# Hedgehog linear attention and Mish layers on one core: first key tiles' sums in twos, block 1's features loaded in stage one, -mean x rstd on GpSimd, statistics behind low parts, fold copies ahead of low parts

## The chip, the cores and the metric

The kernel runs on one core of a Trainium2 chip. The metric is device time in microseconds (us) of one execution; lower is better. The core has TensorE (PE, matmuls), VectorE (DVE), ScalarE (ACT), GpSimd (POOL) and SyncE (SP, which here only issues DMAs). Each engine works through its own queue in order and waits at an instruction until what that instruction needs is there.

## The reference

Two layers, each an attention and a dense block with residuals; 2048 rows of width 640, 32 heads of 20, hidden width 1536, all float32:

```python
for _ in range(2):
    x = x + A(layernorm(x))
    x = x + B(layernorm(x))

def A(x):                      # hedgehog linear attention
    q, k, v = heads(x @ wqkv)
    pq, pk = q @ w_phi, k @ w_phi            # per head, 20 x 20
    phi_q = concat(softmax(pq), softmax(-pq))
    phi_k = concat(softmax(pk), softmax(-pk))
    kv = phi_k.T @ v ; z = sum over rows of phi_k
    return ((phi_q @ kv) / (phi_q @ z + 1e-6)) @ wo

def B(x):                      # dense, Mish, dense
    h = x @ w1 + b1
    return (h * tanh(softplus(h))) @ w2
```

Both layers use the same weights.

## The kernel before

**Numbers.** Matmul operands are split into a high part (rounded to fp32r by an ACT copy) and a low part (the rest, by a subtraction on DVE or GpSimd), and each product is three matmuls: high x high, high x low, low x high. In the profile `xth`/`xtl` are the parts of the transposed rows, `r1h`/`r1l` and `r2h`/`r2l` those of weights.

**Stages.** A layer has three, and TensorE runs through them in turn. Stage one of attention (`attend_first`; about 0 to 246 us in layer 0, 704 to 907 in layer 1) takes the rows in 8 blocks of 256, two tiles of 128 each, tiles 0 to 15. For each tile it makes keys, values and queries by generators (`keys`, `values`, `queries`): a projection of 30 matmuls (L414), an ACT copy out of PSUM, then `features`. That is the two softmaxes: a maximum and a minimum on DVE, two subtractions (one on GpSimd for queries, L440), an exponential on ACT, a row sum and a reciprocal on DVE, and the product with the reciprocal on GpSimd (L450), called the norm product below. From the keys' features and the values (with a column of ones) come the sums phi_k^T V, 32 heads, in a PSUM tile `kva` (L491). Queries' features are transposed on DVE and stored by SP to DRAM, `e_d` (L508), four DMAs per tile. Stage two (`attend_second`) loads `e_d` back (L720, L725), averages (L768), transposes the averages on TensorE (L334, into PSUM tiles called `one`), projects with wo and adds. The dense stage has the two dense products (L892, L943) and the Mish between them.

**Before the first block** of layer 0 the weights of w_phi are folded into those of the keys: `fold_phi` makes pairs of groups on TensorE (L263), and each group's `fold_end` is an ACT copy (`fold_high`, L279) and a DVE subtraction (`fold_low`, L283), group by group.

**Buffers.** Keys' features and loaded `e_d` blocks share a ring of five `big` tiles; pairs of row tiles share a ring of six named `ol`; a query tile is one of two buffers (`r` with number 210 or 211, tile i in i mod 2), which the query tile two later reuses once the store of the former has landed. The first instruction to do so is a small memset (L430) on GpSimd at the head of `features`, or the ACT copy. PSUM has four `one` tiles and two `mm` pairs.

**What sets the order.** A generator's `yield` hands the turn back, and `advance()` gives each pending generator one step, so that the sums of a key tile fall some projections behind its own. In `keys` one more `yield` in the middle blocks puts a block's first tile together with its second, so that 64 heads are summed in one go; the first two and the last blocks sum tile by tile. Inside `written()` and `manual_schedule` instructions stand as the code has them; elsewhere a scheduler orders them within what `tc.issue_after(x)` demands, which is that an instruction stands behind x. `last_low`, `last_sub`, `last_fold` and the like hold such an x: the latest low part, subtraction, fold subtraction. The rows of a block in layer 0 get their layernorm statistics by `norm_stats` (DVE) and `norm_scale` (GpSimd, and -mean x rstd on DVE, L319). In layer 1 these come with the dense stage before; only low parts (L351, on GpSimd there) are left.

**At the end of stage one** `load(0)` and parts of block 1 (`load_groups(1, 0)`, `load_end(1)`) are loaded; `load_groups(1, 5)`, the other half of block 1, is loaded inside stage two, between the stores of query tiles 12 and 13. Query tile 15's copy out of PSUM comes in stage two as well, as the projections left over (`rest`).

Of the kernel before, what the change touches and what calls it, by code (L numbers as in the profile page):

```python
# [8 lines left out]
F32 = mybir.dt.float32  # L9
# [7 lines left out]
P = 128  # L17
S = 2048
D = 640
# [25 lines left out]
def kernel(  # L45
# [45 lines left out]
    for _ in range(30):  # L91
# [25 lines left out]
    last_act, in_written, last_low, last_load, last_recip, last_fold, last_product, last_sub = (  # L117
        [None], [False], [None], [None], [None], [None], [None], [None])
# [20 lines left out]
    def v_tile():  # L139
        return work.tile([P, VW], F32, tag="v", name="v", bufs=2)  # L140

# [144 lines left out]
    def fold_end(ws, ps, k, c):  # L286
        fold_high(ws, ps, k, c)
        fold_low(ws, ps, k, c)

    def fold_phi(ws, bd, raw, parts):  # L290

        for n in range(0, len(parts), 2):
# [6 lines left out]
            for (k, c), ps in pair:  # L299
                fold_end(ws, ps, k, c)  # L300
# [11 lines left out]
    def norm_scale(b, mvs):  # L312

        ve = work.tile([P, BT], F32, tag="ve", name="ve", bufs=2)
        for t in range(BT):
            nc.gpsimd.tensor_scalar(ve[:, t:t + 1], mvs[t][:, 1:2], LN_EPS, 1.0, op0=ALU.add, op1=ALU.mult)
# [108 lines left out]
    def features(ps, e, pool_sub, scale=nc.gpsimd):  # L425
# [23 lines left out]
        last_recip[0] = nc.vector.reciprocal(r, r).ins  # L449
        ins = scale.tensor_tensor(eg, eg, r.unsqueeze(2).to_broadcast([P, 2 * H, DH]), op=ALU.mult).ins  # L450
# [9 lines left out]
    def attend_first(layer, x_src, first):  # L460


        def fetch_normed(b):
# [3 lines left out]
            with (tc.issue_after((last_fold if b == 3 else last_sub)[0]) if b in (1, 3) else nullcontext()):  # L467
# [3 lines left out]
        pending = []  # L471

# [7 lines left out]
        def keys(xts, i, v):  # L480
            e = big_tile()
            yield from features(project(xts, i % BT, kv_ws, 0, w=QC), e, False,
                                nc.vector if i == NT - 1 else nc.gpsimd)
            yield
            if i % BT == 0 and BT < i < NT - BT:
                yield
            for r in range(9):
                for j in range(4):
                    h = 3 * (4 * (r // 3) + j) + r % 3
                    if h < H:  # L490
                        nc.tensor.matmul(kva[32 * j:32 * j + DH + 1, 40 * r:40 * r + 40],  # L491
                                         v[:, (DH + 1) * h:(DH + 1) * (h + 1)], e[:, 40 * h:40 * h + 40],
                                         start=(i == 0 and r == 0), stop=(i == NT - 1), skip_group_check=True)

        def queries(xts, i, ps=None):
# [11 lines left out]
            for q in range(4):  # L507
                nc.sync.dma_start(dst[t, q], e[32 * q:32 * q + 32].rearrange("f (j s) -> f j s", s=32))  # L508
# [3 lines left out]
        def values(xts, i, v):  # L512
            vv = v.rearrange("p (h d) -> p h d", d=DH + 1)
            act(vv[:, :, DH], ident[:, :H], AF.Copy, scale=0.0, bias=1.0)
            if i < BT:
                pv = project(xts, i, kv_ws, D, [one_tile(), one_tile()])
                for c in range(2):
                    act(vv[:, c * H // 2:(c + 1) * H // 2, :DH],
                        pv[c][:, :HC].rearrange("p (h d) -> p h d", d=DH), AF.Copy)
            else:  # L520
                pv = project(xts, i % BT, kv_ws, D)
                act(vv[:, :, :DH].rearrange("p (c h) d -> p c h d", c=2),
# [103 lines left out]
        for b in range(NB):  # L626
# [10 lines left out]
            vs = [v_tile() for _ in range(BT)]  # L637
# [4 lines left out]
            for n, (kind, t) in enumerate(order):  # L642
# [66 lines left out]
        return kva, o_ws, loaded, begun, xs, rest()  # L709
# [5 lines left out]
    def load_groups(b, g0):  # L715
# [5 lines left out]
        return [t[:, g * BLK:(g + 1) * BLK] for g in range(5)]  # L721

# [21 lines left out]
    def attend_second(x_src, x_dst, acc, fetches, makes, fetch_next, begin_next):  # L744
        kva, o_ws, loaded, begun, xs, rest = acc
# [60 lines left out]
        with tc.manual_schedule(engines={mybir.EngineType.PE, mybir.EngineType.SP}):  # L806
            kv = finish_kv(kva)
            next(rest)
            next(kv)
            loaded[1] = begun[0] + load_groups(1, 5) + begun[1]  # L810
# [5 lines left out]
            loaded[2] = load(2)  # L816
# [300 lines left out]
```

## Time and profile before

| | us |
|---|---|
| median of 3 runs | 1357.31 (1357.02 to 1357.4) |
| the profiled execution | 1357.15 |
| its span, first to last instruction | 1355.4 |
| TensorE busy | 1347.9 |
| stage one / two / dense, layer 0 | about 0-250 / 250-356 / 356-704 |
| the same, layer 1 | about 704-911 / 911-1015 / 1015-1356 |

A row of the timeline reads: start, duration, engine, line, operation, result<-operands, shapes, count, and in brackets how long the engine stood idle before it and what ended that. `SPq` rows are issues of DMAs by SP. TensorE overlaps its matmuls: they start closer together than they last.

### The profile page before, as it was taken

To read this page: it belongs to the slowest core of one execution; us is meant where nothing else is said; L and a number is where in the kernel's file an instruction comes from. 1 tells how busy PE (TensorE), PEld (TensorE's weight loads), DVE (VectorE), ACT (ScalarE), POOL (GpSimd) and SP (SyncE) were. 2 spreads that over 40 slices of the span, in tenths; PEclk is the share of its full clock that TensorE was granted. 3 is DMA by queue.
4 is the path that set the end of the run, shared out by engine and by line. 5 is a ranking of instruction groups with operands and counts; after the bars stand their busy time and mean duration, and the time that the engine had idled before them with its cause. 6 is when DMAs were issued, how large, how long until landed. Compare 5 with 4: busy or idle time off the path is not lost.

```text
span 1355.4 us, 30982 instructions
## 1 busy us (share of the span) xinstructions
PE 1347.9 (99%) x12896; PEld 1337.4 (99%) x12896; DVE 1061.2 (78%) x1799; ACT 575.7 (42%) x968; POOL 462.4 (34%) x417
## 2 busy tenths in 40 slices
PE   9999999999999999999999999999999999999999
PEld 9999999999999999999999999999999999999998
DVE  6888988886787887778769788788768776676775
ACT  5444444212454545445443334332236444444443
POOL 3355544334222222222225655634251211111112
PEclk9999999999999999999999999999999999999999
DMA  9544444698714442244474534548974221233200
GB/s 332 166 101 92 95 111 99 173 289 280 216 35 95 117 118 71 61 104 104 140 231 100 122 79 90 95 102 263 282 259 127 79 68 41 88 98 98 70 29 20
DMA packets 352629, 174.11 MB, mean 128 GB/s; under 512 B 287449, under 2 KB 324041, under 8 KB 352489
## 3 DMA queue, kind: packets, MB, share of 16 engines
q1 hardware_dynamic: 352489, 172.14, 46.9%
q8 instruction: 101, 1.65, 0.5%
q14 instruction: 39, 0.32, 0.1%
HBM read 106.23 MB, written 65.86 MB: 127 GB/s over the span
## 4 chain that ended last, share of the span: by engine, by line
PE 94%; DVE 2%; DMA 2%; POOL 1%; SPq 1%; ACT 0%; issue 0%; POOLq 0%; ACTq 0%
PE mm L414 26%; PE one L892 25%; PE mm L943 24%; PE one L414 12%; PE mm L768 2%; PE one L334 2%; PE one L491 1%; PE one L943 1%; DMA xt<-in_x 1%; PE one L768 1%; DVE r L448 1%; DMA raw<-in_wqk_t 0%; DVE m L439 0%; DMA v<-in_wv 0%; DVE r L442 0%; SPq L508 0%
## 5 line engine op out<-in xcount | busy, mean ns | idle before, releaser
L943 PE MATMUL mm<-r2h,ol 128*128 128x320 f32 x1240 | 296.1, 309 | 0.0
L918 POOL TENSOR_TENSOR ol<-big,ol 128x512 fp32r<-128x512 f32 (+1 forms) x98 | 131.1, 1338 | 477.7 <-ACT ol L917 419.5
L892 PE MATMUL one<-xtl,r1h 128*128 128x256 f32 x960 | 268.2, 279 | 0.0
L892 PE MATMUL one<-xth,r1l 128*128 128x256 f32 x960 | 268.0, 279 | 0.0
L892 PE MATMUL one<-xth,r1h 128*128 128x256 f32 x960 | 265.9, 279 | 0.0
L943 PEld LDWEIGHTS mm<-r2h,ol 128*128 128x128 f32 x1240 | 212.5, 188 | 0.0
L943 PE MATMUL mm<-r2l,ol 128*128 128x320 f32 x620 | 191.2, 309 | 0.0
L414 PE MATMUL mm<-r1h,xth 128*128 128x304 f32 (+1 forms) x600 | 185.2, 309 | 0.0
L414 PE MATMUL mm<-r1l,xth 128*128 128x304 f32 (+1 forms) x600 | 183.7, 306 | 0.0
L414 PE MATMUL mm<-r1h,xtl 128*128 128x304 f32 (+1 forms) x600 | 183.6, 306 | 0.2 <-POOL xtl L351 0.2
L892 PEld LDWEIGHTS one<-xtl,r1h 128*128 128x128 f32 x960 | 180.4, 188 | 0.0
L892 PEld LDWEIGHTS one<-xth,r1l 128*128 128x128 f32 x960 | 180.4, 188 | 0.0
L892 PEld LDWEIGHTS one<-xth,r1h 128*128 128x128 f32 x960 | 179.6, 188 | 0.0
L907 DVE TENSOR_SCALAR big<-big 128x512 f32<-128x512 f32 (+1 forms) x98 | 57.2, 583 | 110.0 <-ACT big L905 109.8
L909 ACT ACTIVATE big<-big,two 128x512 f32<-128x512 f32 (+1 forms) x98 | 70.1, 715 | 116.1 <-DVE big L908 116.1
L917 ACT ACTIVATE ol<-big 128x512 fp32r<-128x512 f32 (+1 forms) x98 | 60.9, 622 | 137.6 <-DVE big L916 137.4
L905 ACT ACTIVATE big<-one,b1s 128x256 f32<-128x256 f32 x192 | 80.9, 468 | 89.0 <-PE one L892 88.5
L450 POOL TENSOR_TENSOR r<-r,r 128x1280 f32<-128x1280 f32 x32 | 77.2, 2413 | 118.9 <-DVE r L449 100.8
L943 PEld LDWEIGHTS mm<-r2l,ol 128*128 128x128 f32 x620 | 116.4, 188 | 0.0
L414 PEld LDWEIGHTS mm<-r1h,xth 128*128 128x128 f32 x600 | 112.8, 188 | 0.9
L414 PEld LDWEIGHTS mm<-r1h,xtl 128*128 128x128 f32 x600 | 112.8, 188 | 0.4 <-POOL xtl L351 0.4
L414 PEld LDWEIGHTS mm<-r1l,xth 128*128 128x128 f32 x600 | 112.8, 188 | 0.1
(161 smaller groups left out, 3142.7 us busy)
## 6 DMA issues: line engine op xcount, KB each, us to landing
e_d<-r SPq DMA_DIRECT2D x128, 160.0 KB, 4.2
big<-e_d SPq DMA_DIRECT2D x32, 640.0 KB, 8.0
x_d<-xt SPq DMA_DIRECT2D x23, 640.0 KB, 4.8
xt<-x_d SPq DMA_DIRECT2D x22, 640.0 KB, 5.3
n_d<-xn SPq DMA_DIRECT2D x168, 80.0 KB, 2.3
xt<-in_x SPq DMA_DIRECT2D x16, 640.0 KB, 4.4
xn<-x_d SPq DMA_DIRECT2D x28, 320.0 KB, 4.4
v<-n_d SPq DMA_DIRECT2D x30, 256.0 KB, 3.0
```

What stands on the lines that cost most here:

```text
L334: nc.tensor.transpose(ps[:, c, t * P:(t + 1) * P], self.rows[t][:, (c0 + c) * P:(c0 + c + 1) * P], ident)
L414: last_product[0] = nc.tensor.matmul(ps[:, :w], a[:, sl], r, start=(k == 0 and n == 0), stop=(k == KD - 1 and n == 2)).ins
L448: nc.vector.tensor_reduce(r, eg, axis=AX.X, op=ALU.add)
L450: ins = scale.tensor_tensor(eg, eg, r.unsqueeze(2).to_broadcast([P, 2 * H, DH]), op=ALU.mult).ins
L768: nc.tensor.matmul(po[c][64 * q:64 * q + 64, GW * j:GW * j + w], phs[g][:n, s0:s0 + 64], kvb[:n, g, :w], start=True, stop=True)
L892: nc.tensor.matmul(ph[:, j, :], l, r, start=(n == 0), stop=(n == 3 * KD - 1))
L905: exps[0] = nc.scalar.activation(part(ta, 0)[:, j - js.start], ph[:, j, :], AF.Exp, bias=b1s[:, 2 * pr + j:2 * pr + j + 1]).ins
L907: nc.vector.tensor_scalar_min(e, e, E_CAP)
L909: nc.scalar.activation(r, n, AF.Ln, bias=two)
L917: nc.scalar.activation(ah[:, js], n, AF.Copy)
L918: nc.gpsimd.tensor_tensor(al[:, js], n, ah[:, js].bitcast(F32), op=ALU.subtract)
L943: ins = nc.tensor.matmul(pys[t][c][:, :HC], (ah, ah, al)[n][:, j, t * P:(t + 1) * P], w, start=(f == 0 and n == 0), stop=(f == KF - 1 and ...
```

## The change

Five edits. (1) The sums of the first two blocks are also made for two tiles at once: `held(i)` gives the number of extra `yield`s for tile i. For this the values of block 0 (layer 0) and of block 2 (layer 1) come in two halves out of the `ol` ring (`v_halves`), written by two copies each. (2) The features of block 1 are loaded wholly in stage one, one big tile and three `ol` tiles (`load_rest`), and block 2's load stands behind the last store of tile 13 (`last_store`). (3) -mean x rstd is a `tensor_scalar` on GpSimd outside `written()`. (4) In `fold_phi` both high copies stand ahead of both subtractions. (5) The next block's statistics stand behind the last low part; in block 1 of layer 1 the keys' features take one more `yield`, and their norm product stands behind the low parts (`late`).

```diff
@@ features, keys
+        if late:
+            yield
         r = work.tile([P, 2 * H], F32, tag="r", name="r", bufs=2)
...
-        ins = scale.tensor_tensor(eg, eg, r.unsqueeze(2).to_broadcast([P, 2 * H, DH]), op=ALU.mult).ins
+        with (tc.issue_after(last_low[0]) if late else nullcontext()):
+            ins = scale.tensor_tensor(eg, eg, r.unsqueeze(2).to_broadcast([P, 2 * H, DH]), op=ALU.mult).ins
...
-            with (tc.issue_after((last_fold if b == 3 else last_sub)[0]) if b in (1, 3) else nullcontext()):
+            with tc.issue_after((last_sub if b == 1 else last_low)[0]):
                 norm_scale(b, [norm_stats(t, xt) for t in range(BT)])
...
+        def held(i):
+
+            b, t = divmod(i, BT)
+            if layer and b == 1:
+                return (3, 2)[t]
+            if b == 1 or (b == 0 and not layer):
+                return (2, 0)[t]
+            return int(t == 0 and b < NB - 1)
...
-                                nc.vector if i == NT - 1 else nc.gpsimd)
+                                nc.vector if i == NT - 1 else nc.gpsimd, layer and i // BT == 1)
             yield
-            if i % BT == 0 and BT < i < NT - BT:
+            for _ in range(held(i)):
                 yield
+            opens = not summed[0]
+            summed[0] = True
...
-                                         v[:, (DH + 1) * h:(DH + 1) * (h + 1)], e[:, 40 * h:40 * h + 40],
-                                         start=(i == 0 and r == 0), stop=(i == NT - 1), skip_group_check=True)
+                                         v[1][c][:, (DH + 1) * g:(DH + 1) * (g + 1)], e[:, 40 * h:40 * h + 40],
+                                         start=(opens and r == 0), stop=(i == NT - 1), skip_group_check=True)
@@ values
-            vs = [v_tile() for _ in range(BT)]
+            vs = [v_halves(b == 2 * layer) for _ in range(BT)]
+    def v_halves(apart):
+
+        if apart:
+            return None, [pair_tile(F32).rearrange("p a s -> p (a s)")[:, :VW // 2] for _ in range(2)]
+        v = v_tile()
+        return v, [v[:, :VW // 2], v[:, VW // 2:]]
@@ norm_scale, fold_phi
-            nc.vector.scalar_tensor_tensor(stats[:, b, 1, t:t + 1], mvs[t][:, 0:1], -1.0,
-                                           stats[:, b, 0, t:t + 1], op0=ALU.mult, op1=ALU.mult)
+            (nc.vector if in_written[0] else nc.gpsimd).tensor_scalar(
+                stats[:, b, 1, t:t + 1], mvs[t][:, 0:1], stats[:, b, 0, t:t + 1], -1.0, op0=ALU.mult, op1=ALU.mult)
...
-            for (k, c), ps in pair:
-                fold_end(ws, ps, k, c)
+            for end in (fold_high, fold_low):
+                for (k, c), ps in pair:
+                    end(ws, ps, k, c)
@@ loads
-                    begun = load_groups(1, 0), load_end(1)
+                    loaded[1] = load_groups(1, 0) + load_rest(1)
+    def load_rest(b):
+
+        out = []
+        for g0 in (5, 7, 9):
+            t = pair_tile(F32)
+            n = min(2, 10 - g0)
+            src = e_d[b][120 * g0:120 * (g0 + n - 1) + P]
+            src = bass.AP(tensor=src.tensor, offset=src.offset, ap=[[BLK, P], [120 * BLK, n], [1, BLK]])
+            nc.sync.dma_start(t[:, :n], src)
+            out += [t[:, 0], t[:, 1]]
+        nc.sync.dma_start(t[:80, 1], e_d[b][1200:])
+        return out
...
             next(rest)
+            with tc.issue_after(last_store[0]):
+                loaded[2] = load(2)
             next(kv)
-            loaded[1] = begun[0] + load_groups(1, 5) + begun[1]
             next(kv)
             next(rest)
             average(0, 0)
             average(0, 1)
             next(rest)
-            loaded[2] = load(2)
```

Lines of the changed kernel are some 4 to 34 higher than those of the kernel before (L279 becomes L286, L351 L355, L430 L434, L440 L444, L450 L457, L508 L528, L720 L741, L725 L759).

How the order moves at three places. First ACT at the weights' fold of layer 0 (`r1h0` to `r1h3` are the high copies, `xn` the rows normalised for block 1, `v` and `ol` the values), before:

```order
L279 ACTIVATE r1h0_166<-mm_420 128x342
L279 ACTIVATE r1h2_170<-mm_431 128x342
L279 ACTIVATE r1h1_168<-mm_420 128x342
L135 ACTIVATE xn_442<-xt_198,stats_113 128x640
L135 ACTIVATE xn_443<-xt_198,stats_113 128x640
L135 ACTIVATE v_358<-ident_70 128x32
L135 ACTIVATE v_358<-one_447 128x16x20
L279 ACTIVATE r1h3_172<-mm_431 128x342
```

and after:

```order
L286 ACTIVATE r1h0_166<-mm_423 128x342
L286 ACTIVATE r1h1_168<-mm_423 128x342
L286 ACTIVATE r1h2_170<-mm_434 128x342
L286 ACTIVATE r1h3_172<-mm_434 128x342
L135 ACTIVATE xn_445<-xt_198,stats_113 128x640
L135 ACTIVATE xn_446<-xt_198,stats_113 128x640
```

The fourth copy moves from behind the normalisations to ahead of them.

Second, SP where stage one of layer 0 goes over into stage two (`e_d0`, `e_d1` and so on are the blocks in DRAM; `r210` and `r211` hold query tiles 12 and 13), before:

```order
L720 DMA big_3113<-e_d0_116 128x5x256
L720 DMA big_3117<-e_d1_117 128x5x256
L508 DMA e_d6_122<-r210_2829 32x40x32 x4
L720 DMA big_3298<-e_d1_117 128x5x256
L508 DMA e_d6_122<-r211_2874 32x40x32 x4
L720 DMA big_3386<-e_d2_118 128x5x256
```

and after:

```order
L741 DMA big_3117<-e_d0_116 128x5x256
L741 DMA big_3121<-e_d1_117 128x5x256
L528 DMA e_d6_122<-r210_2833 32x40x32 x4
L528 DMA e_d6_122<-r211_2878 32x40x32 x4
L741 DMA big_3305<-e_d2_118 128x5x256
L741 DMA big_3307<-e_d2_118 128x5x256
```

The load between the two stores is gone; the other half of block 1 is among the loads far ahead of this place.

Third, GpSimd in blocks 1 and 2 of layer 1 (`xtl` low parts; `r210`, `r211` query tiles; `big_9235`, `big_9307` and in the other kernel `big_9242`, `big_9282` the keys of block 1; `big_9607`, and `big_9584` and `big_9624`, those of block 2), before:

```order
L450 TENSOR_TENSOR r211_9184<-r211_9184,r_9422 128x1280
L351 TENSOR_TENSOR xtl_9433<-xn_9229,xth_9431 128x512
L450 TENSOR_TENSOR big_9235<-big_9235,r_9469 128x1280
L430 MEMSET r210_9482 128x32
L351 TENSOR_TENSOR xtl_9480<-xn_9231,xth_9478 128x512
L450 TENSOR_TENSOR big_9307<-big_9307,r_9516 128x1280
L351 TENSOR_TENSOR xtl_9522<-xn_9233,xth_9520 128x256
L440 TENSOR_TENSOR r210_9482<-r210_9482,m_9558 128x32x20
```

and after:

```order
L457 TENSOR_TENSOR r211_9191<-r211_9191,r_9429 128x1280
L355 TENSOR_TENSOR xtl_9440<-xn_9236,xth_9438 128x512
L434 MEMSET r210_9485 128x32
L355 TENSOR_TENSOR xtl_9483<-xn_9238,xth_9481 128x512
L457 TENSOR_TENSOR big_9242<-big_9242,r_9519 128x1280
L355 TENSOR_TENSOR xtl_9525<-xn_9240,xth_9523 128x256
L457 TENSOR_TENSOR big_9282<-big_9282,r_9566 128x1280
L444 TENSOR_TENSOR r210_9485<-r210_9485,m_9561 128x32x20
```

The memset of the query tile is now the second of these behind `r211`, and the two norm products of the keys are behind the second and the last low part. In block 2, after:

```order
L355 TENSOR_TENSOR xtl_9833<-xn_9580,xth_9831 128x512
L457 TENSOR_TENSOR big_9584<-big_9584,r_9758 128x1280
L434 MEMSET r210_9835 128x32
L457 TENSOR_TENSOR big_9624<-big_9624,r_9869 128x1280
L355 TENSOR_TENSOR xtl_9875<-xn_9582,xth_9873 128x256
```

The second norm product stands behind a memset and ahead of the last low part; before, the last low part was ahead of it.

More of the change, by code (lines that the diff above doesn't have):

```diff
@@ L423, in query_tile, with features @@
         return r2_wide(10 + i % 2, F32).rearrange("p s d -> p (s d)")
-    def features(ps, e, pool_sub, scale=nc.gpsimd):
+    def features(ps, e, pool_sub, scale=nc.gpsimd, late=False):
         eg = e.rearrange("p (g d) -> p g d", d=DH)
@@ L707, in rest @@
                 advance()
-        return kva, o_ws, loaded, begun, xs, rest()
+        return kva, o_ws, loaded, xs, rest()
     def load(b):
```

28 lines of the change are left out of this document (14 added, 14 removed).

## The prediction

> **What bounds the kernel now.** I read the page's header first, then the chain of waits, then the list of what TensorE waited for, then the windows by stage.
>
> ```profile
> span 1355.4 us, 30982 instructions
> PE 1347.9 (99%) x12896; PEld 1337.4 (99%) x12896; DVE 1061.2 (78%) x1799; ACT 575.7 (42%) x968; POOL 462.4 (34%) x417
> PE 94%; DVE 2%; DMA 2%; POOL 1%; SPq 1%; ACT 0%; issue 0%; POOLq 0%; ACTq 0%
> PE one L334 <- ACT r L135: 1.8, 2, 1.3
> PE mm L263 <- DVE r1l L283: 0.4, 1, 0.4
> PE mm L414 <- POOL xtl L351: 0.2, 1, 0.2
> 0.00:250.00 250.00, 248.04 (x2756) 244.61 (x2758) 208.18 (x306) 108.92 (x168) 116.21 (x115) 1.00 0.54 141
> 356.00:704.00 348.00, 348.00 (x2665) 348.00 (x2664) 280.01 (x487) 175.10 (x310) 82.09 (x81) 1.00 0.42 110
> ```
>
> TensorE is the bound: 1347.9 of 1355.4 us busy, and 94% of the chain that ended last. The next three rows list waits (us in total, times, longest); the last two are windows (length, then busy time of PE, weight loads, DVE, ACT, POOL, then the granted clock, 1.00). The first dense stage has no idle microsecond at all, so nothing that moves there can gain. Only two things shorten this kernel: fewer or cheaper TensorE instructions, and the waits in the list. The change takes up three of its entries, 2.4 us together, and the cost of four switches between two shapes of matmul. An edit on another engine counts only where it makes TensorE wait.
>
> **The weights' fold.** Both ACT copies of a pair of groups now stand ahead of both DVE low parts.
>
> ```profile
> 29.73 0.46 ACT L279 ACTIVATE r1h<-mm 128x342 fp32r<-128x342 f32 x1 [2.14 <-DVE r1l L283]
> 30.09 1.72 ACT L135 ACTIVATE xn<-xt,stats 128x640 f32<-128x640 f32 x2
> 32.15 0.45 ACT L279 ACTIVATE r1h<-mm 128x342 fp32r<-128x342 f32 x1
> 32.63 0.52 DVE L283 TENSOR_TENSOR r1l<-mm,r1h 128x342 fp32r<-128x342 f32 x1 [1.40 <-ACT r1h L279]
> 33.29 0.64 PE L263 MATMUL mm<-big,raw 120*128 120x114 f32 x4 [0.38 <-DVE r1l L283]
> ```
>
> The third copy (29.73) waited 2.14 us for a low part, so two normalisations (1.72 us) slipped ahead of the fourth (32.15); its low part ended at 33.15 and the matmul that takes its buffer lost 0.38. With the four copies in a row the fourth ends some 4 us earlier, far ahead of TensorE. A stall also breaks the overlap of matmuls, which start 0.14 apart and last 0.30 (next fence): another 0.16. So **0.54 saved**; bounds 0.38 and 0.54. The normalisations slip by two copies (0.9 us) and TensorE needs their result only in block 1.
>
> **The sums in twos.** A group of sums stands between projections, single (64 instructions) or for two tiles (128):
>
> ```profile
> 725.97 0.30 PE L414 MATMUL mm<-r1h,xtl 128*128 128x304 f32 x1
> 726.21 0.83 PE L491 MATMUL one<-big,v 128*21 128x40 f32 x64
> ...
> 727.22 0.31 PE L414 MATMUL mm<-r1l,xth 128*128 128x320 f32 x1
> ...
> 776.12 0.30 PE L414 MATMUL mm<-r1l,xth 128*128 128x304 f32 x1
> 776.26 0.30 PE L414 MATMUL mm<-r1h,xtl 128*128 128x304 f32 x1
> 776.49 1.48 PE L491 MATMUL one<-big,v 128*21 128x40 f32 x128
> ...
> 778.14 0.30 PE L414 MATMUL mm<-r1l,xth 128*128 128x304 f32 x1
> ```
>
> From the last projection before to the second behind pass 1.25 us for a single and 1.88 for a pair. Either stretch holds two ordinary steps of 0.14, so the excursion costs 0.96 or 1.60, and a merge of two singles saves 2 x 0.96 - 1.60 = 0.32. Layer 0 merges twice: **0.64**. Layer 1 merges twice, but its second pair is parted again, 9 instructions at one place and the rest 16 projections on, which gives one merge back: **0.32**. The Trainium skill says the same of the direction (TensorEngine Tiling (Array Packing), Key Properties): changing the tiling mode drains TensorE. Its rule has no figure, and the rows give 0.32.
>
> The later sums must not wait for their products. In layer 0 the second pair moves ahead to about 86.3 us, since its place is 423 projections into the stage. GpSimd's queue there holds the product row below, which ended at 87.12 against a single sum at 87.7; three small statistics and a memset (2.0 us in all) leave its way, so I put it at 85.1 to 85.4: a slack of about 0.9 us, and no wait.
>
> ```profile
> 84.75 2.37 POOL L450 TENSOR_TENSOR big<-big,r 128x1280 f32<-128x1280 f32 x1
> ```
>
> The values' halves cost ACT two more copies of ones and, in layer 1, one more copy of values per tile. ACT is 42% busy and such copies are under 0.8 us: nothing.
>
> **The stage boundary of layer 0.** This is the largest term.
>
> ```profile
> 236.05 3.34 SPq L508 DMA_DIRECT2D e_d<-r  x4
> 245.27 0.38 SPq L720 DMA_DIRECT2D big<-e_d  x1
> 245.75 7.23 SPq L508 DMA_DIRECT2D e_d<-r  x4
> 243.30 1.50 DVE L503 STREAM_TRANSPOSE r<-r 128x1280 f32<-128x1280 f32 x1
> 255.44 0.74 ACT L135 ACTIVATE r<-one 128x304 f32<-128x304 f32 x2 [5.16 <-DMA e_d<-r]
> 253.55 1.09 PE L334 MATMUL one<-ident,xn 128*128 128x128 f32 x8
> 255.92 0.44 PE L334 MATMUL one<-ident,xn 128*128 128x128 f32 x2 [1.28 <-ACT r L135]
> 256.71 0.69 DVE L351 TENSOR_TENSOR xtl<-one,xth 128x512 fp32r<-128x512 f32 x1 [1.48 <-ACT xth L135]
> ```
>
> The last query tile's copy (ACT, 255.44) overwrites the buffer of tile 13 and waited 5.16 us for that tile's store; TensorE's ninth transpose needs the PSUM tile that this copy frees, 0.48 us later. Tile 13 was transposed at 244.80, but its four stores stood on SP behind a load of block 1's features (245.27), which itself waits for the last pair of sums, and shared the DMA engines with it: 7.23 us to issue instead of 3.34. The change takes that load away; block 1's features come in during the stage, in one big tile and four smaller DMAs of the same bytes, and block 2's load stands behind the stores.
>
> Now the first store issues at about 244.85. If it lands 9.7 us later as here (245.75 to 255.44), the transpose starts at 255.03; if the issue takes 3.9 us less, at 251 or so, which is no limit. The eight transposes cost (1.09 - 0.27)/7 = 0.117 each from start to start (0.27 the length of one), so the ninth could start at 254.49. The gain is 0.89 to 1.43; I take **1.43**, as the store at 236.05, without a load ahead, is the nearest row. DVE's 1.48 idle goes with it, and it is the engine that the next TensorE work follows.
>
> **The same place in layer 1.**
>
> ```profile
> 906.75 5.75 SPq L508 DMA_DIRECT2D e_d<-r  x4
> 916.49 0.44 PE L334 MATMUL one<-ident,xn 128*128 128x128 f32 x2 [0.53 <-ACT r L135]
> ```
>
> Here 0.53 + 0.16 = **0.69** can go; the stores begin only some 0.2 us earlier, so the low bound is 0.2, the high one 0.69 with the shorter issue.
>
> **Layer 1's stage one: GpSimd.** Here the change also costs.
>
> ```profile
> 742.38 0.68 ACT L135 ACTIVATE r<-mm 128x608 f32<-128x608 f32 x1 [3.93 <-DMA e_d<-r]
> 746.72 0.74 POOL L351 TENSOR_TENSOR xtl<-xn,xth 128x256 fp32r<-128x256 f32 x1
> 747.51 0.41 PE L414 MATMUL mm<-r1h,xtl 128*128 128x304 f32 x1 [0.15 <-POOL xtl L351]
> 769.97 0.55 DVE L449 RECIPROCAL r<-r 128x64 f32<-128x64 f32 x1
> 771.47 2.37 POOL L450 TENSOR_TENSOR big<-big,r 128x1280 f32<-128x1280 f32 x1
> ```
>
> Block 2's last low part ended at 747.46 behind two norm products; TensorE lost 0.15 + 0.16 = 0.31. Now only one product stands ahead of it, but so does the query tile's memset, which waits for a store that landed by 742.38 (ACT waited for the same). Taking a landing near 741.3 (the DVE work ahead of its transpose gets about 1 us shorter): low part 1.29, product 2.37, low part 0.74, ready at 745.8. TensorE has passed three singles here before, one pair now, 2.88 - 1.60 = 1.28, and asks at 747.36 - 1.28 = 746.1. So **0.31 saved**; with the landing at 742.38 it is 0.7 late, and nothing is saved.
>
> What is late next: both keys' products of block 1 follow, the second ends near 748.2 and the queries' subtraction behind it starts 0.8 us later than now; and in block 2 DVE takes both reciprocals only behind both reductions and transposes. I work the first to 769.8, near the row at 769.97. GpSimd then needs two products, start to start 2.33, and between them a memset that waits for a store: ready at about 774.5. The row above ended at 773.84, and TensorE asked at 776.49. It now asks 16 projections earlier (2.24), one excursion of 0.64 and the 0.31 less: 773.2. A **new wait of 1.1**; bounds 0 and 2.4 (both products as now, or a store as late as the row at 742.38).
>
> **Statistics.** They move behind low parts, and -mean x rstd to GpSimd: about 0.46 us for two, by this row of the same kind.
>
> ```profile
> 26.28 0.46 POOL L316 TENSOR_SCALAR ve<-mv 128x1 f32<-128x1 f32 x2 [3.10 <-DVE mv L309]
> ```
>
> It lies ahead of normalisations that have a whole block to come; in the dense stages the window above shows no gap to lose or win. Uncovered it would be 0.46 per block, 2.8 for six blocks.
>
> **The sum** against the profiled execution (1357.15 us, 1355.4 of span and 1.75 around it): 0.54 + 0.64 + 0.32 + 1.43 + 0.69 + 0.31 - 1.1 = 2.83, so 1354.3. The median of the runs shown is 1357.31, 0.16 above that execution. The new wait is the softest term, and a part of it was reckoned with dense engines; I say **1354.2**. By the bounds the gain is 0.38 + 0.64 + 0.32 + 0.89 + 0.2 + 0 - 2.4 = 0.0 at the worst and 3.93 at best; they will not all fall together, so the likeliest case's own range is 1353.2 to 1355.6.
>
> **Rivals.**
> - *The boundary stays late* (the stores still land 9.7 us after issue, in both layers): 1.43 and 0.69 become 0.89 and 0.2 less what block 2's load, now right behind the stores, adds. With neither gained at all, 0.71 remains: 1356.5. For it speaks the DMA share of 0.54 in the first window; against it the 3.34 us of the store at 236.05.
> - *GpSimd blocks DVE in layer 1.* A DVE operation beside a norm product takes far longer:
>
> ```profile
> 722.09 2.97 DVE L442 TENSOR_TENSOR r<-m,r 128x640 f32<-128x640 f32 x1 [0.20 <-POOL r L440]
> 748.72 0.82 DVE L442 TENSOR_TENSOR r<-m,r 128x640 f32<-128x640 f32 x1 [3.92 <-POOL r L440]
> ```
>
>  The late products fall beside such subtractions: 2.15 us per meeting, one of them on the way to block 2's pair, makes the new wait 1.1 + 1.5 = 2.6: a gain of 1.3, 1355.8. The Trainium skill has the rule (SBUF — State Buffer, SBUF: two separate sides): GpSimd and a DVE operation with two SBUF inputs take a shared port pair as an exclusive lock, and the loser blocks wholly; this trace agrees, with 2.97 against 0.82.
> - *Slower: memsets in GpSimd's queue.* A query tile's memset that waits for a store now stands ahead of products or low parts whose slack I put at 0.9 us (layer 0, second pair), 0.3 (the low part at 745.8) and none (block 2's pair). If stores land 3.9 us late, as the issue of 7.23 against 3.34 shows they can, these cost 3.0, 3.6 and some 2 more: 8.6 against gains of 3.6, about 1362. It is slower than before from about 2 us of lateness at all three. Against it: no store in the middle of a stage was issued so slowly.
> - *The change doesn't do what it says*: besides the parted pair, already in the sum, I see no place in the order where this holds.
>
> **Chances.** 0.2% is 2.7 us, about what a measurement of this kernel can tell from no change; faster means below 1354.6. The likeliest case has 0.70 (0.58 below that line, 0.12 above), the late boundary 0.08, the blocked DVE 0.11, the slower one 0.11. So faster 0.58, same 0.31, slower 0.11. The range reaches from 1353.0 to 1357.2 and leaves out the slower case and a little at the low end.
>
> **What would show it.** Right: no idle time ahead of TensorE's fold matmul, the ninth transpose or the last low part; groups of 128 sums at the first two blocks; the four stores issued ahead of the load in under 5 us. Wrong: a TensorE wait for a norm product at the second pair of layer 0 or block 2's in layer 1 of over 2.4 us, or an ACT copy of the last query tile that still waits for a store beyond 254 us.

## The result and the profile after

The changed kernel takes 1353.61 us in the median of 9 runs (1353.13 to 1354.08), the kernel before in the same series 1357.02 (9 runs, 1356.33 to 1358.99). The ratio is 0.9974 with a 95% interval of 0.9964 to 0.9984: 3.4 us faster. The prediction was 1354.2, with a range of 1353.0 to 1357.2.

The header, TensorE's waits (us in total, times, longest) and two windows of the changed kernel, in the columns of the prediction's:

```profile
span 1352.1 us, 31029 instructions
PE 1346.0 (100%) x12896; PEld 1337.5 (99%) x12896; DVE 1040.4 (77%) x1737; ACT 576.6 (43%) x974; POOL 480.6 (36%) x479
PE mm L418 <- ACT r L135: 1.1, 1, 1.1
PE mm L418 <- POOL xtl L355: 0.2, 1, 0.2
0.00:250.00 250.00, 248.49 (x2780) 246.06 (x2781) 206.48 (x296) 110.12 (x170) 120.27 (x129) 1.00 0.55 143
704.00:911.00 207.00, 205.71 (x2447) 202.95 (x2445) 171.93 (x194) 79.90 (x118) 114.99 (x89) 1.00 0.48 100
```

Waits of the first 15 us, which both kernels have, are left out. The waits that the change aimed at are gone: those at the fold, at the ninth transpose of both boundaries, and at block 2's low part (747.51 before; the 0.2 that still stands here is at another low part, at 772.28). A new one stands in the list: TensorE waits 1.1 us for a query tile's copy. In layer 1's stage one (704 to 911) TensorE is busy for 205.71 us where it was 206.84: that stage has become worse.

**Where the time went, by stage.** Both kernels run the same 3840 projection matmuls in stage one and two in the same order of places, so the n-th of them can be matched. The lead below is the start of the n-th in the kernel before minus its start in the other kernel; a column is the lead's change over a stretch, and the last the whole lead at the last one. The column of layer 0's boundary holds the dense stage behind it as well. Between the 2701st and the 3301st the lead changes by 0.03 us at most, but for two kernels below.

| kernel | at the 1st | fold (to 126th) | rest of stage one, layer 0 (to 1401st) | boundary, layer 0 (to 1951st) | stage one, layer 1 (to 2701st) | boundary, layer 1 (3301st to 3601st) | lead |
|---|---|---|---|---|---|---|---|
| predicted | 0 | 0.54 | 0.64 | 1.43 | -0.47 | 0.69 | 2.83 |
| changed | 0.05 | 0.75 | 0.47 | 1.63 | -0.97 | 1.22 | 3.14 |
| changed, again (below) | 0.28 | 0.75 | 0.45 | 1.62 | -0.94 | 1.18 | 3.37 |

In these two executions the stages repeat within 0.04 us; the lead at the very first projection moves from run to run. It is 0.0 to 0.95 over all kernels run here, and so a single span says little below one microsecond, while a stage's share says more. Two cautions go with the shares. All of them are taken against one execution of the kernel before, and its own waits vary: the first experiment shows 0.41 and 0.32 at boundaries that its kernel leaves alone. And where TensorE runs close to a store, the share varies too: the kernel without layer 1's merges, run twice below, has -0.14 and -0.01 in layer 1's stage one.

The fold and the boundary of layer 0 in the changed kernel, rows of the timeline:

```profile
27.09 0.80 ACT L286 ACTIVATE r1h<-mm 128x342 fp32r<-128x342 f32 x2 [0.34 <-PE mm L270]
28.11 1.74 ACT L135 ACTIVATE xn<-xt,stats 128x640 f32<-128x640 f32 x2 [0.21 <-POOL stats L323]
29.08 0.87 DVE L290 TENSOR_TENSOR r1l<-mm,r1h 128x342 fp32r<-128x342 f32 x2
32.60 0.61 PE L270 MATMUL mm<-big,raw 120*128 120x114 f32 x4
...
235.84 11.90 SPq L528 DMA_DIRECT2D e_d<-r  x6
247.86 1.74 SPq L741 DMA_DIRECT2D big<-e_d  x2
250.69 0.74 ACT L135 ACTIVATE r<-one 128x304 f32<-128x304 f32 x2 [1.66 <-DMA e_d<-r]
252.29 1.31 PE L338 MATMUL one<-ident,xn 128*128 128x128 f32 x10
```

The fourth high copy ends at 27.89 and its low part, which frees the buffer, at 29.95, more than two microseconds ahead of the matmul that wants it (32.60), which no longer waits. At the boundary SP issues the stores (grouped with those of the tile before) up to 247.74 and only then the load; the last query tile's copy runs at 250.69 where it ran at 255.44, and the ten transposes stand in one row without a gap.

### The profile page after: what moved, and what is told of

It reads as the page before. It is cut to its first block, busy times and chain, and to the rows that moved or that the text cites. A ratio compares the mean times of both kernels' runs of the same rounds, so it can differ in the third digit from the quotient of the medians.

```text
span 1352.1 us, 31029 instructions
## 1 busy us (share of the span) xinstructions
PE 1346.0 (100%) x12896; PEld 1337.5 (99%) x12896; DVE 1040.4 (77%) x1737; ACT 576.6 (43%) x974; POOL 480.6 (36%) x479
## 5 line engine op out<-in xcount | busy, mean ns | idle before, releaser
L457 POOL TENSOR_TENSOR r<-r,r 128x1280 f32<-128x1280 f32 x32 | 77.4, 2420 | 112.3 <-DVE r L455 88.9
```

## The experiments

Each kernel's table row has the columns of the table above.

**The fold alone.** The kernel before with both copies ahead of both subtractions.

```diff
-            for (k, c), ps in pair:
-                fold_end(ws, ps, k, c)
+            for end in (fold_high, fold_low):
+                for (k, c), ps in pair:
+                    end(ws, ps, k, c)
```

> The kernel before with the fold's order alone: both high copies ahead of both low parts. Theory A (each part of the change pays by the wait it removes): TensorE has no idle time ahead of its fold matmul at 33 us, and from there to the end runs 0.54 to 0.6 us ahead of the kernel before; every other wait of before (1.28 at the boundary of layer 0, 0.53 in layer 1, 0.15 at the low part) stays as it is. Rival: the wait passes on to the next block's normalised rows, which stand behind the copies, and the lead at 60 us is under 0.2 us.

Measured: 0.32 at the first projection, then 0.75, -0.04, 0.41, 0.04 and 0.32 by stage; the span is 1354.0. The fold gives 0.75 and all but 0.04 of it is kept through stage one, so the rival falls. The 0.41 and 0.32 at the boundaries, where this kernel changes nothing, are a measure of the traces: the wait of 1.28 was 0.76 here, since the store landed sooner, and in layer 1 four averages (L768) took 0.27 us, which in the profile of before, with nothing that they wait for, took 0.60 at 914.34. Against this a gap of 0.28 us that nothing shown ends, at 832 us, takes 0.43 from the lead.

**The loads alone.** The kernel before with block 1 loaded in stage one and block 2's load behind the stores (`load_rest`, `last_store`).

```diff
-                    begun = load_groups(1, 0), load_end(1)
+                    loaded[1] = load_groups(1, 0) + load_rest(1)
...
-            loaded[1] = begun[0] + load_groups(1, 5) + begun[1]
...
+            with tc.issue_after(last_store[0]):
+                loaded[2] = load(2)
```

> The kernel before with the loads' part alone: block 1's features loaded in stage one, block 2's load behind the stores. Theory A: the wait for the last query tile's copy goes in both layers, and with it the two waits of 0.2 us some 23 us later; TensorE's lead is 1.4 to 1.7 us behind the boundary of layer 0 and 2.4 to 2.9 us at the end; the four stores of tile 13 issue in under 4.5 us. Rival (the stores are late because the DMA engines are full in this stretch, whatever stands ahead on SP): they still take over 6 us to issue and the lead behind the boundary of layer 0 is under 0.9 us.

Measured: -0.44 in the fold, -0.40, **1.49** at the boundary of layer 0, 0.00, and **1.07** at that of layer 1; span 1353.5. The rows of its boundary:

```profile
236.89 12.98 SPq L508 DMA_DIRECT2D e_d<-r  x8
249.99 1.54 SPq L721 DMA_DIRECT2D big<-e_d  x2
252.80 0.74 ACT L135 ACTIVATE r<-one 128x304 f32<-128x304 f32 x2 [1.67 <-DMA e_d<-r]
```

The first row holds two tiles; tile 13's four stores in it issue from 245.71 to 249.88, in 4.17 us where it was 7.23. The wait for the copy is gone in both layers, so the rival falls: it was the load ahead on SP that made the store late. Two parts were wrong. The waits some 23 us behind the boundaries stayed, as 0.07 us of idle time each, with 0.14 lost against the changed kernel. And the lead at the end is 1.7, not 2.4 to 2.9, for two losses in stage one of layer 0. The -0.44 shows how unsteady the fold of before is: here it lost time at two matmuls (0.30 and 0.38 us idle), not at one. The -0.40 is a wait at 140.10 (0.13 us idle) for a query tile's copy that itself waited for a store; the kernel before did not wait there.

**-mean x rstd on DVE again**, in the changed kernel.

```diff
-            (nc.vector if in_written[0] else nc.gpsimd).tensor_scalar(
-                stats[:, b, 1, t:t + 1], mvs[t][:, 0:1], stats[:, b, 0, t:t + 1], -1.0, op0=ALU.mult, op1=ALU.mult)
+            nc.vector.scalar_tensor_tensor(stats[:, b, 1, t:t + 1], mvs[t][:, 0:1], -1.0,
+                                           stats[:, b, 0, t:t + 1], op0=ALU.mult, op1=ALU.mult)
```

> The changed kernel with -mean x rstd on DVE again. Theory A (DVE is the last engine ahead of TensorE in stage two, so the two small instructions per block count there): the wait of before at the first projection behind the transposes of stage two (about 275 and 936 us) is back in both layers with 0.1 to 0.2 us of idle time, and all else is as in the changed kernel: the lead at the end is 0.2 to 0.4 us smaller. Rival (those waits went with the stage boundary's, which sets the pace of DVE there): no wait at these places, and the lead is as in the changed kernel within 0.1.

Measured: 0.75, 0.45, 1.51, -0.63, 1.06. Against the changed kernel the boundaries lose 0.12 and 0.16, and both waits are back, smaller than expected (0.06 us idle, 0.13 to 0.14 lost). So moving two small instructions off DVE gains 0.28 us in stage two (0.23 against the second execution of the changed kernel). The lead at the end was 4.0, not smaller, because the first projection was 0.83 us ahead and the store that layer 1 waits for landed earlier in this run (a wait of 0.8 in place of 1.1); that stage holds nothing of this edit, so its -0.63 against -0.97 shows how far a stage with a wait for a store varies.

**Layer 1's merges undone**, layer 0 as changed.

```diff
             if layer and b == 1:
-                return (3, 2)[t]
-            if b == 1 or (b == 0 and not layer):
+                return 0
+            if (b == 1 or b == 0) and not layer:
                 return (2, 0)[t]
-            return int(t == 0 and b < NB - 1)
+            return int(t == 0 and 1 < b < NB - 1)
...
-                                nc.vector if i == NT - 1 else nc.gpsimd, layer and i // BT == 1)
+                                nc.vector if i == NT - 1 else nc.gpsimd)
...
-            vs = [v_halves(b == 2 * layer) for _ in range(BT)]
+            vs = [v_halves(b == 0 and not layer) for _ in range(BT)]
```

> The changed kernel with layer 1's sums, values and norm products as before (layer 0 as changed). Theory A (in layer 1 the merges make TensorE early for a query tile's store and cost more than they save, 0.96 us net): no wait at 769 to 773 us, the 0.15 at the low part of block 2 is back, TensorE is 2.9 us ahead of the kernel before at 900 us and about 4.1 at the end; the span is about 1351.2. Rival (the waits of layer 1 come with the norms on GpSimd or with what else moved, not with the merges): they stay, and without the merges' gain the span is 1352.4 or more.

Measured: 0.75, 0.47, 1.62, **-0.14**, 1.22; span 1351.0. The waits at 769 to 773 us go with the merges, one of 0.09 us idle for a copy is left at 774.8, and the 0.15 at the low part is back. Theory A holds: in layer 1 the merges, with what was moved for them, cost 0.83 us net (0.96 by the second execution of this kernel, below). Why they cost is the subject of the next kernels.

**A tile of its own for query tile 4** of layer 1.

```diff
-    def query_tile(i):
+    def query_tile(i, spare=False):
+        if spare:
+            return x_tile().rearrange("p t d -> p (t d)")
...
-            e = query_tile(i)
+            e = query_tile(i, layer and i == 4)
```

> The changed kernel with query tile 4 of layer 1 in a tile of its own (a free tile of the rows' ring), so that its copy out of PSUM waits for no store. Theory A: the 1.10 us wait at 769.5 goes, but the last low part of block 2, behind the second norm product on GpSimd, is now what is late: TensorE waits there 1.2 to 1.7 us instead of 0.2, and the lead at 800 us stays 1.9 to 2.4. Rival (the store is the only cause): both waits go, or the second stays at 0.2; the lead at 800 us is 3.2 or more and the span about 1350.8.

First the changed kernel at this place, ACT, GpSimd and TensorE:

```profile
768.80 0.68 ACT L135 ACTIVATE r<-mm 128x608 f32<-128x608 f32 x1 [6.23 <-DMA e_d<-r]
769.54 0.41 PE L418 MATMUL mm<-r1h,xth 128*128 128x304 f32 x1 [1.10 <-ACT r L135]
769.17 2.37 POOL L457 TENSOR_TENSOR big<-big,r 128x1280 f32<-128x1280 f32 x1
771.69 0.39 PE L511 MATMUL one<-big,ol 128*21 128x40 f32 x18
772.28 0.41 PE L418 MATMUL mm<-r1h,xtl 128*128 128x304 f32 x1 [0.20 <-POOL xtl L355]
```

The copy waited for the store of the tile two before it, the projection for the copy's PSUM pair. The norm product was ready at 771.54, just in time for the sums at 771.69. Now the kernel with a tile of its own:

```profile
770.87 0.40 PE L513 MATMUL one<-big,ol 128*21 128x40 f32 x18 [0.94 <-POOL big L459]
771.55 0.41 PE L418 MATMUL mm<-r1h,xtl 128*128 128x304 f32 x1 [0.29 <-POOL xtl L355]
```

The wait for the store is gone, and TensorE waits at the norm product of the parted pair instead (0.94), then at the low part (0.29): 0.88 lost in the stage up to the 2701st projection against 0.97. That the time moves to GpSimd's queue is what theory A said; the place in it was the product, not the low part. Later in the stage this kernel lost another 1.5 us at copies of later query tiles (1.28 and 0.10 us idle), the larger one behind a store, which neither theory expected; what delayed that store was not followed up.

**One merge of two in layer 1**: block 0's pair kept, block 1 as before.

```diff
             if layer and b == 1:
-                return (3, 2)[t]
+                return 0
```

> The changed kernel with layer 1 merging block 0's sums only; block 1's sums single, its norm products and values as before. Theory A (early in layer 1 TensorE can't run further ahead than GpSimd's low parts and the query tiles' stores let it): the merge's 0.32 us shows up to 740 us and is then lost at the last low part of block 2, whose wait grows from 0.15 to 0.4 or more; the lead at 800 us is that of the kernel without any merge in layer 1, within 0.15. Rival (merges in layer 1 pay by themselves, and the norm product behind the low parts is what hurts): the lead at 800 us is 0.25 to 0.4 larger than without.

Block 1's norm products and values are as before too; these two lines of the edit are not shown. Measured: 0.75, 0.47, 1.62, **-0.38**, 1.22. Not even one merge pays: it costs 0.24 against none (0.37 by the second execution of that kernel), though its own 0.3 are there. TensorE waits 0.84 us for the low part. GpSimd's rows show why:

```profile
737.35 0.16 POOL L434 MEMSET r<- 128x32 f32 x1 [1.75 <-DMA e_d<-r]
737.43 2.38 POOL L457 TENSOR_TENSOR big<-big,r 128x1280 f32<-128x1280 f32 x1
739.76 1.29 POOL L355 TENSOR_TENSOR xtl<-xn,xth 128x512 fp32r<-128x512 f32 x1
741.00 2.37 POOL L457 TENSOR_TENSOR big<-big,r 128x1280 f32<-128x1280 f32 x1
743.33 0.72 POOL L355 TENSOR_TENSOR xtl<-xn,xth 128x256 fp32r<-128x256 f32 x1
744.11 0.41 PE L418 MATMUL mm<-r1h,xtl 128*128 128x304 f32 x1 [0.84 <-POOL xtl L355]
```

With the merge the scheduler puts the query tile's memset ahead of the first norm product; it waits 1.75 us for a store, and all that stands behind it comes that much later. In the kernel without merges the product stands first and the memset waits for nothing:

```profile
737.53 2.37 POOL L457 TENSOR_TENSOR big<-big,r 128x1280 f32<-128x1280 f32 x1
739.84 0.16 POOL L434 MEMSET r<- 128x32 f32 x1
```

**The norm products of block 1 not behind the low parts**, merges as in the change (one more `yield` in `held` stands for the one that `late` made).

```diff
             if layer and b == 1:
-                return (3, 2)[t]
+                return (4, 3)[t]
...
-                                nc.vector if i == NT - 1 else nc.gpsimd, layer and i // BT == 1)
+                                nc.vector if i == NT - 1 else nc.gpsimd)
```

> The changed kernel with block 1's norm products in layer 1 where they were, not behind the low parts; the sums merged as in the change. Theory A: TensorE waits 1.5 to 2.3 us for the last low part at 743 us, which has the memset and both products ahead of it, and then not or under 0.5 at 769 us, since it is that much later; the lead at 800 us is 1.4 to 2.2, so the step behind the low parts only chose at which of the two places the time is lost. Rival (the products behind the low parts made the query tile's store late): the wait at 743 us is under 0.6, none at 769 us, and the lead at 800 us is over 2.8.

Measured: 0.76, 0.47, 1.63, **-1.54**, 1.20.

```profile
743.88 0.32 PE L511 MATMUL one<-big,v 128*21 128x40 f32 x10 [1.22 <-POOL big L457]
744.57 0.41 PE L418 MATMUL mm<-r1h,xtl 128*128 128x304 f32 x1 [0.36 <-POOL xtl L355]
```

As theory A has it, the time is lost at 743 us and nothing at 769. The scheduler parted block 1's pair as well, so that most of the loss shows up at a product. The change's step behind the low parts is worth 0.57 us here; it chose the cheaper of two places.

**The changed kernel and its best variants, timed together.** First the changed kernel again.

> The changed kernel again, beside the variants below on one chip. The stages' shares of its lead over the kernel before repeat within 0.3 us: 0.75 in the fold, 0.47 in the rest of layer 0's stage one, 1.63 at its boundary, -0.6 to -1.0 in layer 1's stage one, 1.1 to 1.2 at the last boundary; the lead at the first projection may be anything from 0 to 1.

Measured: median 1353.66 of 9 runs (1353.31 to 1354.46) against 1356.94 before; its row stands in the table above.

Then the kernel without layer 1's merges again.

> Again the changed kernel without the merges of layer 1, timed. Theory A (they cost 0.8 us net): median 0.5 to 1.1 us below the changed kernel's in this same series. Rival (the single execution was a good one): within 0.3 us of it.

Measured: median 1352.46 of 6 runs (1352.13 to 1353.44), 1.2 below the changed kernel, ratio to before 0.9968 (0.9956 to 0.9980); layer 1's stage -0.01. So the lower time of the single execution above was no accident.

Then the same with the last low part made one step earlier in block 1 of layer 1, ahead of the second norm product:

```diff
                     elif n > 2:
-                        nxt.step()
+                        for _ in range((1, 2, 0)[n - 3] if layer and b == 1 else 1):
+                            nxt.step()
```

> The kernel without merges in layer 1, and block 2's last low part made one step earlier there, ahead of block 1's second norm product on GpSimd. Theory A (behind the low part the query tiles' stores are the next limit, with no slack): the wait of 0.15 at 744 us goes, but what it gave shows up as 0.2 to 0.3 us of wait for a query tile's copy at 768 to 775 us; the lead at 800 us is within 0.15 of the kernel without this step. Rival (the low part was the only limit): the lead grows by 0.3 and stays.

Measured: layer 1's stage **0.43**, median 1352.42 of 5 runs (1352.03 to 1352.78). No wait of TensorE is left anywhere behind the fold. Here the rival was right: the low part was the only limit, and the stores had slack. That theory A missed says that being early does not by itself run into the stores. The median is that of the kernel without the step; 0.4 us is below what these series tell apart, and only the stage's share shows it.

Then block 0's merge with the earlier low part.

> Block 0's merge in layer 1 and the earlier low part together. Theory A: no wait at 744 us, and 0.3 to 0.9 us of waits for a query tile's copy between 768 and 776; layer 1's stage one gains less than 0.15 us in all. Rival: it gains 0.5 to 0.65 (0.32 by the merge and 0.31 by the low part).

Measured: layer 1's stage **-0.02**, with 0.51 us idle at 774.6 for a query tile's copy. As expected in size, but after the kernel before it the reason had to be another: the merge had brought the waiting memset back (1.97 us). So the last kernel holds that memset behind the first norm product, with `last_norm` the latest of these, and is otherwise the same.

```diff
-        nc.gpsimd.memset(eh[:, 1, :, DL:], 0.0)
+        with (tc.issue_after(last_norm[0]) if behind else nullcontext()):
+            nc.gpsimd.memset(eh[:, 1, :, DL:], 0.0)
...
-            yield from features(project(xts, i % BT, q_ws, 0, w=QC) if ps is None else ps, e, True)
+            yield from features(project(xts, i % BT, q_ws, 0, w=QC) if ps is None else ps, e, True,
+                                behind=layer and i == 2)
```

> Block 0's merge and the earlier low part in layer 1, as in the kernel before this one, and the memset of the first query tile of block 1 held behind block 1's first norm product on GpSimd (with the merge it had moved ahead of it and waited 1.97 us for a store). Theory A (what a merge in layer 1 costs is this memset's wait at the head of GpSimd's queue, by which the query tiles' stores come late): the memset waits for nothing, the wait of 0.5 us at 774.6 is gone or under 0.15, and layer 1's stage one gains 0.6 to 0.75 us, 0.43 of the low part and 0.32 of the merge; the median is 1352.0 to 1352.4. Rival (TensorE is simply too far ahead for the stores, whatever the memset does): the wait at 774 us stays at 0.3 or more and the stage gains under 0.45.

Measured: layer 1's stage **0.72**, median 1351.78 of 5 runs (1351.61 to 1352.31) against 1356.88 before in its series, ratio 0.9966 (0.9952 to 0.9979).

```profile
736.67 2.37 POOL L458 TENSOR_TENSOR big<-big,r 128x1280 f32<-128x1280 f32 x1 [0.80 <-DVE r L456]
738.98 0.16 POOL L435 MEMSET r<- 128x32 f32 x1
739.05 2.00 POOL L355 TENSOR_TENSOR xtl<-xn,xth 128x512 fp32r<-128x512 f32 x2
772.49 0.68 ACT L135 ACTIVATE r<-mm 128x608 f32<-128x608 f32 x1 [5.42 <-DMA e_d<-r]
773.66 0.41 PE L418 MATMUL mm<-r1h,xth 128*128 128x304 f32 x1
```

The memset waits for nothing, the copy is done in time, and TensorE has no gap. Both gains are there in full, 0.43 and 0.29. So what block 0's merge cost in layer 1 was the memset ahead of the norm products, not TensorE's being early. The change itself has that memset in the same place, waiting 1.92 us; with its second merge as well the remedy was not tried. It is also the lowest median of all kernels tried; its series is not that of the kernels above, but the kernel before reads within 0.1 us in both.

## Why the prediction was right, step by step

- **What bounds the kernel** held: each gain is a wait of TensorE that went or switches that it no longer makes, and the dense stages gave nothing. The lead is the same to 0.03 us from 287 to 700. That the total came so near is in part luck: layer 1's stage one came out 0.50 worse than reckoned and the last boundary 0.53 better, for unrelated reasons that follow.
- **The fold**, 0.54 predicted, gave 0.75. The wait and its lost overlap are 0.57 of it. Another 0.10 is a delay at the matmuls just before (31.38), which I had not counted, and 0.08 comes behind the fold, where the eight transposes in a row of before now stand as four and four. The direction and place were right.
- **The sums in twos in layer 0**, 0.64 predicted, gave 0.47 with all else in that stage. The second merge gave its 0.32 in full (the lead goes from 1.00 to 1.31 between the 360th and the 430th projection), the first 0.21, and 0.05 went in small steps over the rest of the stage, as 0.04 did with the fold alone. The step that was mis-sized is the price of the first pair's excursions. Both its singles stood right beside transposes, and the four transposes of one group behind a single (63.21) now stand among projections in two groups (63.18 and 64.03); the prediction charged each single the 0.96 of one that stands between projections. That this is the reason is read from the order in the traces and was not tried. The second pair had its products in time: GpSimd was done at 85.72 (I had put 85.1 to 85.4; the product took 2.97 us, not 2.37), and the pair began at 86.20.
- **The boundary of layer 0**, 1.43 predicted, gave 1.63: 1.49 by the loads alone, 0.12 by the smaller load on DVE. The copy ran at 250.69, where I had put the store's landing at about 251. Both shares are against the one execution of the kernel before in which TensorE waited 1.28 there; with the 0.76 of the first experiment's execution they would be some 0.4 smaller. So the mechanism held, and the size held for that execution.
- **The same place in layer 1**, 0.69 predicted, gave 1.22. Of this 0.16 is DVE's, and 0.3 the stall in the averages, which only the profile of before has; the first experiment, with no change there, shows 0.32 for it. About 0.74 remains for the wait itself.
- **Layer 1's stage one**, -0.47 predicted, -0.97 measured. The merges and the low part came in: at the 2402nd projection, with the four singles of before and both pairs passed, the lead has grown from 2.87 to 3.91, by 1.04 (0.31 and 0.30 for the merges, 0.43 for the low part) where 0.64 and 0.31 were reckoned. The parted pair of block 2 then takes its share, about 0.3, as worked out (18 of its 128 sums stand ahead, not 9). The new wait is where the prediction's step failed. I had it at block 2's norm product, 1.1 us (my own figures give 1.2: ready at 774.5, asked for at 773.3); TensorE lost 1.36 at the store of a query tile and then about 0.3 behind the second product on GpSimd. With the store's wait taken away the product's wait appears with 0.94 us, so the working of that queue was near the truth, but it was not the wait that ends last. Ahead of both stands what I had named as a rival and put at no cost in the sum: the memset that waits for a store, here 1.92 us, at the head of GpSimd's queue.

```profile
735.21 1.30 POOL L355 TENSOR_TENSOR xtl<-xn,xth 128x512 fp32r<-128x512 f32 x1
738.42 0.16 POOL L434 MEMSET r<- 128x32 f32 x1 [1.92 <-DMA e_d<-r]
738.50 1.29 POOL L355 TENSOR_TENSOR xtl<-xn,xth 128x512 fp32r<-128x512 f32 x1
```

How the store came late can be read from the two traces. TensorE came to the copy's place 3.9 us earlier than before. The queries' subtraction on GpSimd came only 2.3 us earlier (745.11, was 747.41), the first of the store's four issues 1.2 (762.13, was 763.36) and the copy 0.9 (768.80, was 769.71). So 1.6 us were lost up to GpSimd's subtraction, where the memset had waited, and 1.1 more between it and the store, on DVE. There a subtraction that stood behind the tile's transpose now stands ahead of it, beside a low part on GpSimd; the changed kernel's row and that of before:

```profile
759.24 1.44 DVE L446 TENSOR_TENSOR big<-m,big 128x640 f32<-128x640 f32 x1
763.26 0.78 DVE L442 TENSOR_TENSOR big<-m,big 128x640 f32<-128x640 f32 x1
```

With both merges in place neither share was tried by a run of its own.

- **Statistics and -mean x rstd**, predicted at nothing, gained 0.23 to 0.28: DVE is what TensorE follows in stage two, and the list of waits had no row for it because each wait was under 0.1 us of idle time. Their cost on GpSimd was hidden, as worked out: stage one of layer 0 has 0.47 with them there and 0.45 without.
- **The rivals.** The late boundary did not happen: the stores land sooner once the load is not ahead of them. The slower case's mechanism did happen, at one place and with 1.9 us instead of 3.9, and cost layer 1 its merges; the gains elsewhere outweighed it. The parted pair is as the order showed it. The rival by which GpSimd blocks DVE was not tried by itself; in the changed kernel's trace it may have the 0.66 us by which the subtraction at 759.24 is longer than that of before, on the way to the late store.

## What to carry to other kernels

An instruction that only prepares a buffer still stands in its engine's queue: put ahead of real work and waiting for a store, a memset of 0.16 us cost a stage more than the edit around it saved. When an edit makes the busiest engine early, look on every engine that feeds it for what stands at the head of the queue and waits, and test each place of an edit by itself: here the good parts hid one that lost 0.8 to 1.0 us. Where both kernels run the same instructions, match them one by one and compare stages: in the changed kernel and its variants a stage without a wait for a store repeated to 0.04 us when whole runs differed by one. Take more than one execution of the kernel before, since one of its waits alone moved by half a microsecond.

## What the runs showed of the hardware

The start of the kernel is the noisiest part of it: in kernels with the same code ahead of it the first projection began between 12.6 and 13.5 us after the first instruction. What sets this was not followed up. Going from the projections' shape of matmul to that of the sums and back cost 0.96 us with 64 sums and 1.60 with 128. Putting two singles together gave 0.30 to 0.32 each time where they stood among projections, and 0.21 where they stood beside transposes. Of one wait of the kernel before, that for the store at the boundary of layer 0, two executions showed 1.28 and 0.76 us with the same order of instructions there.
